# Retention and feed-forward in one kernel: items of a block taken as two, three and three instead of two at a time

## The chip, the cores and the metric

The kernel runs on one core of one Trainium2 chip. The metric is device microseconds of one execution. The core's engines are named as in the profile: PE (TensorE, matrix products; PEld is its loading of weights), DVE (VectorE), ACT (ScalarE), POOL (GpSimd) and SP (SyncE, which here issues nearly all DMAs). PE writes its results to PSUM, which has eight banks of 128 partitions x 512 fp32 values; DVE and ACT read them from there into SBUF.

## The reference, cut to what matters

```python
B, H, S, D = 8, 8, 576, 64
scores = matmul(q, k.transpose(0, 1, 3, 2)) / sqrt(D)
gamma = 1.0 - 2.0 ** (-5.0 - arange(H))
rel = arange(S)[:, None] - arange(S)[None, :]
Dmat = where(rel >= 0, gamma[:, None, None] ** rel, 0.0)
x = matmul(scores * Dmat, v)              # (B, H, S, D)
x = x.transpose(0, 2, 1, 3).reshape(B * S, H * D)     # 4608 x 512
h = x @ w_in                              # 512 x 2048
out = (h - tanh(h)) @ w_out               # 2048 x 512
```

All inputs are fp32. It is attention whose weights are scores times a decay that depends on the head and the distance, and a feed-forward layer behind it.

## The kernel before

**Blocks and items.** The sequence of 576 is cut into nine chunks of 64 positions. A *block* n is chunk n of all eight sequences: 512 tokens. An *item* j = 8 n + b is one sequence's chunk, with its eight heads: q, k, v and k by rows, 4 x 64 columns on 128 partitions each (two heads on top of each other). The decay is put into tables, so that within a block the scores need only a causal mask, and what earlier chunks contribute is one 64x64 *state* for each head, which grows by k'v of each chunk.

**The retention of an item** is three sorts of small products, each of 64x64 quarters of PE's array: *scores* (`m_score`, L220, 8 program matmuls), *states* (`m_state`, L226, 8) and *outputs* (`m_out`, L237, 16: state times q, and masked scores times v). Scores and states use the two quarters on the diagonal, outputs the two others; `run` (L247) issues two of the one and two of the other sort in turn, so that four quarters are at work. The profile shows every such matmul as two instructions.

**An entry** (`entry`, L289) does this for a pair of items: scores of the next pair, outputs and states of this one. Then DVE masks the scores (`after_score`, L255), ACT and DVE split the outputs into two words xh and xl (`after_out`, L276), DVE adds the states (L311), SP loads the pair after next (`load_pair`, L163, 1 MB, two buffers of the tag `a`), and POOL scales its q and v by tables (`prep`, L178). The table for q changes with the block: `load_qtab` (L155) loads it into one buffer.

**The feed-forward layer.** For block n and one of sixteen slices f of the inner dimension, `mm1(n, f)` (L320) makes h in a bank of the tag `h` (two buffers) with 12 matmuls of 128x128 by 512 columns: four parts of the contraction, and three products each, because weights and x are held as a high and a low word. `activate` (L345) turns h into g = h - tanh(h), again as two words gh and gl: tanh on ACT, subtraction on DVE, cast on ACT, subtraction on DVE. `mm2(n, f)` (L381) adds this slice's part of the result into four banks o0 to o3 with 12 matmuls. They go by word first (all of gh, then gl), except in a block's last mm2, where they go by bank, so that each bank is stored as it ends: `store` (L400) copies o0 and o2 on ACT, o1 and o3 on DVE, into tiles of the tag `cv` (three buffers), and SP stores them.

**The order of the work** is written out by hand, and `in_order` holds every engine's instructions to it. Each engine, and SP's queue of DMAs, does its instructions in that order and waits at one whose inputs or buffers aren't ready. It has three parts:

- The start and the loop over `seq` (L529): items of chunk 0, then mm1 of blocks 0 and 1 while the weights are loaded and converted. The 32 weight tiles arrive as 64-bit words of which the kernel makes two fp32 words (`guard`, L91: a mask, by tanh and abs on ACT; `unit`, L100: three bit operations on DVE, a cast on ACT, a subtraction on DVE). Entries for block 1 stand behind k = 5, 8, 10 and 14. h of both blocks is spilled to DRAM.
- The loop over `late` (L570): mm2 of block 1 and then of block 0, 32 in all, k from 0 to 31. Iteration k issues `words` for k + 1 (cast on ACT, subtraction on DVE, into gh and gl of two buffers each), `resume` for k + 2 (tanh on ACT, subtraction on DVE), the `fetch` for k + 4 on SP (256 KB from DRAM, three buffers of the tag `g`), what is left of the conversions, and mm2 of k. Block 1's last mm2, with its stores, is k = 15. Entries for block 2 stand ahead of mm2 at k = 3, 8, 13 and 18.
- The loop over blocks 2 to 8 (L586): mm1(n, f), then the mm2 of one f earlier; behind mm1 at f = 1, 5, 9 and 13 stands an entry for the next block, and the list `todo` holds what mm2 is still due.

Of the kernel before, what the change touches and what calls it, by code (L numbers as in the profile page):

```python
# [19 lines left out]
P = 128  # L20
NF = DF // P
NCC = DM // P
C = 64
# [4 lines left out]
HI_BITS = float(0x3FFFFF80)  # L28
# [5 lines left out]
NP = NC * B // 2  # L34
# [33 lines left out]
def retention_ffn(ctx: ExitStack, tc: tile.TileContext, ins, out, spill):  # L68
# [84 lines left out]
    loaded, scored, xs, qtabs = {}, {}, {}, {}  # L153
# [9 lines left out]
    def load_pair(p, u=None):  # L163

        if p >= NP:
            return
        c, pr = divmod(p, B // 2)
        load_qtab(c)
        a = loaded["pair", p] if u == 1 else pool.tile([P, 2, 4, 4, C], F32, tag="a", name=f"a{p}")
        if u is None:  # L170
            nc.sync.dma_start(a, qkv_d[c - 1, 2 * pr : 2 * pr + 2].rearrange("u p t i s -> p u t i s"))
        else:
            nc.sync.dma_start(a[:, u], qkv_d[c - 1, 2 * pr + u])
        loaded[2 * p], loaded[2 * p + 1] = a[:, 0], a[:, 1]
        loaded["pair", p] = a
        loaded["qv", p] = a[:, :, 0], a[:, :, 2]

    def prep(p, q=True):  # L178
        if p >= NP:
            return  # L180
        c = p // (B // 2)
        a = loaded["pair", p]
        if q:
            table = qtabs[c].unsqueeze(1).broadcast_to([P, 2, 4, C])
            nc.gpsimd.tensor_tensor(a[:, :, 0], a[:, :, 0], table, op=ALU.mult)  # L185
        nc.gpsimd.tensor_tensor(  # L186
            a[:, :, 2], a[:, :, 2], vtab[:, c].unsqueeze(1).unsqueeze(3).broadcast_to([P, 2, 4, D]), op=ALU.mult
        )

    def load_early(p):
        c, pr = divmod(p, B // 2)
        if pr < 2:
            return load_pair(p)
        src = qkv_d[c - 1, 2 * pr : 2 * pr + 2].rearrange("u p t i s -> p u t i s")
        parts = []
        for t in range(2):
            parts.append(const.tile([P, 2, 2, 4, C], F32, tag=f"wo{2 * (pr - 2) + t}", name=f"a_early{p}_{t}"))
            nc.sync.dma_start(parts[t], src[:, :, 2 * t : 2 * t + 2])  # L200
            behind(tc, pace[-1])
        for u in range(2):
            loaded[2 * p + u] = Parts([part[:, u] for part in parts])
        loaded["qv", p] = parts[0][:, :, 0], parts[1][:, :, 0]

    def scale_q(p):
        q, table = loaded["qv", p][0], qtabs[p // (B // 2)]
        nc.vector.tensor_tensor(q, q, table.unsqueeze(1).broadcast_to([P, 2, 4, C]), op=ALU.mult)

    def scale_v(p):  # L210
        v = loaded["qv", p][1]
# [25 lines left out]
    def m_out(j, o):  # L237
# [17 lines left out]
    def after_score(j, sc, n):  # L255
# [5 lines left out]
        else:  # L261
            pm = pool.tile([P, 2, 4, C], F32, tag="pm", bufs=1, name=f"pm{j}")
            nc.vector.tensor_tensor(
                pm[:, :n].rearrange("p u i q -> p (u i) q"), sc.rearrange("p u i q -> p (u i) q"),
                mask.unsqueeze(1).broadcast_to([P, 4 * n, C]), op=ALU.mult,
# [388 lines left out]
```

## Time and profile before

| | us |
|---|---|
| median of 3 runs | 891.48 (889.31 to 891.55) |
| the profiled execution | 891.8 |
| its span, first to last instruction | 890.0 |
| PE busy | 877.6 (99%) |
| PEld busy | 724.3 (81%) |
| DVE busy | 363.3 (41%) |
| ACT busy | 287.7 (32%) |
| POOL busy | 67.7 (8%) |
| granted PE clock, mean | 0.995 of full speed |

Times in rows are microseconds from the first instruction, and a row's second number is how long it took; groups show the mean of one in ns. An engine's row names the line, the operation, the tiles (out<-in) and their shapes; in brackets stands how long the engine stood idle before it and what ended that. A busy PE is not PE at its peak: matmuls overlap, and the distance from one start to the next is the price, not the length of the row.

### The profile page before, as it was taken

Reading aid. Unit: us, or ns where it says so; the run is one execution under the profiler, and the core shown is the slowest. Engines: PE = TensorE matmul, PEld = TensorE weight load, DVE = VectorE, ACT = ScalarE, POOL = GpSimd, SP = SyncE. Lnnn points to the kernel's source line nnn. Section 1 sums busy time; section 2 is a strip of 40 time slices with the busy share of each in tenths; the row PEclk is TensorE's granted clock in tenths of the full one; section 3 lists DMA queues with packets and bytes.
Section 4 is the critical chain, followed back from the end, with each engine's and each line's share of the span. In section 5 each row is a group of like instructions: output and inputs, shape, how many; then the busy total and the mean of one; then the engine's idle time right before and its main releaser. Section 6 shows DMA issues by size and latency. Waiting matters only on the chain.

```text
span 890.0 us, 17595 instructions
## 1 busy us (share of the span) xinstructions
PE 877.6 (99%) x7848; PEld 724.3 (81%) x7848; DVE 363.3 (41%) x548; ACT 287.7 (32%) x503; POOL 67.7 (8%) x59
## 2 busy tenths in 40 slices
PE   7999999999999999999999999999999999999997
PEld 6777878788888888888888888888888888888886
DVE  6879777653432332333233233323323322222222
ACT  4887774443222222222222222222222221222222
POOL 0001001210111110111111111111000111000000
PEclk8999999999999999999999999999999999999999
DMA  9966965551311131102111131113111201002001
GB/s 354 325 231 212 342 193 171 167 167 48 96 54 49 48 96 49 54 30 68 47 54 49 49 95 54 49 48 96 49 54 47 62 35 48 1 1 49 1 1 47
DMA packets 31372, 82.06 MB, mean 92 GB/s; under 512 B 3776, under 2 KB 4928, under 8 KB 31296
## 3 DMA queue, kind: packets, MB, share of 16 engines
q1 hardware_dynamic: 30768, 80.02, 27.8%
q8 instruction: 61, 1.00, 0.5%
q10 hardware_dynamic: 528, 0.92, 0.3%
q14 instruction: 15, 0.12, 0.0%
HBM read 63.62 MB, written 17.30 MB: 91 GB/s over the span
## 4 chain that ended last, share of the span: by engine, by line
PE 90%; DMA 3%; DVE 3%; ACT 2%; issue 0%; SPq 0%; DVEq 0%
PE o L393 44%; PE h L327 38%; PE s L252 3%; DMA rwo<-in_w_out_dram 2%; PE new L252 2%; PE own L252 2%; DMA rwi<-in_w_in_dram 1%; DVE mo L110 0%; DVE mo L112 0%; ACT mi L95 0%; ACT mi L98 0%; PE new_first L252 0%; DVE mi L105 0%; DVE wi L124 0%; ACT wi L117 0%
## 5 line engine op out<-in xcount | busy, mean ns | idle before, releaser
L327 PE MATMUL h<-xh,wi 128*128 128x512 f32 x1152 | 307.0, 392 | 2.7 <-ACT g L339 0.8
L393 PE MATMUL o<-wo,gh 128*128 128x512 f32 x1144 | 291.6, 393 | 0.4 <-DVE ob L412 0.4
L327 PEld LDWEIGHTS h<-xh,wi 128*128 128x128 f32 x1152 | 216.3, 189 | 49.7 <-ACT g L339 1.3
L393 PEld LDWEIGHTS o<-wo,gh 128*128 128x128 f32 x1144 | 212.3, 188 | 46.8 <-DVE ob L412 1.5
L354 DVE TENSOR_TENSOR g<-h,g 128x512 f32<-128x512 f32 x114 | 78.8, 691 | 367.1 <-ACT g L353 367.1
L353 ACT ACTIVATE g<-h 128x512 f32<-128x512 f32 x114 | 68.3, 599 | 420.9 <-PE h L327 420.1
L393 PE MATMUL o<-wo,gl 128*128 128x512 f32 x572 | 157.3, 389 | 0.0
L327 PE MATMUL h<-xl,wi 128*128 128x512 f32 x576 | 154.5, 390 | 0.0
L327 PEld LDWEIGHTS h<-xl,wi 128*128 128x128 f32 x576 | 108.7, 189 | 22.9
L393 PEld LDWEIGHTS o<-wo,gl 128*128 128x128 f32 x572 | 107.4, 188 | 22.3
L356 DVE TENSOR_TENSOR gl<-g,gh 128x512 fp32r<-128x512 f32 x113 | 81.0, 717 | 77.5 <-ACT gh L355 70.0
L355 ACT CAST gh<-g 128x512 fp32r<-128x512 f32 x113 | 70.1, 620 | 86.2 <-DVE g L354 86.2
L185 POOL TENSOR_TENSOR a<-a,qtab 128x512 f32<-128x512 f32 x27 | 36.3, 1344 | 605.7 <-DMA a<-in_qkv_dram 547.3
L252 PE MATMUL own<-a,state 64*64 64x64 f32 x960 | 58.9, 221 | 0.0
L252 PE MATMUL own<-pm,a 64*64 64x64 f32 x960 | 57.5, 218 | 0.0
L252 PEld LDWEIGHTS own<-a,state 64*64 64x64 f32 x960 | 47.8, 134 | 0.4 <-issue 0.4
L252 PEld LDWEIGHTS own<-pm,a 64*64 64x64 f32 x960 | 48.0, 135 | 0.0
L252 PEld LDWEIGHTS s<-a 64*64 64x64 f32 x960 | 30.3, 134 | 10.6 <-issue 10.2
L186 POOL TENSOR_TENSOR a<-a,vtab 128x512 f32<-128x512 f32 x28 | 32.2, 1152 | 67.4 <-DVE mi L112 67.4
L252 PE MATMUL s<-a 64*64 64x64 f32 x960 | 34.4, 221 | 0.0
L376 DVE TENSOR_TENSOR gl<-s,gh 128x512 fp32r<-128x512 f32 x30 | 21.6, 720 | 31.2 <-PE o L393 24.4
L375 ACT CAST gh<-s 128x512 fp32r<-128x512 f32 x30 | 18.6, 621 | 39.0 <-PE o L393 27.4
(67 smaller groups left out, 465.0 us busy)
## 6 DMA issues: line engine op xcount, KB each, us to landing
a<-in_qkv_dram SPq DMA_DIRECT2D x29, 1024.0 KB, 5.2
out_dram<-ob SPq DMA_DIRECT2D x69, 128.0 KB, 2.4
rwi<-in_w_in_dram SPq DMA_DIRECT2D x16, 512.0 KB, 5.8
rwo<-in_w_out_dram SPq DMA_DIRECT2D x16, 512.0 KB, 5.1
s<-spill_dram SPq DMA_DIRECT2D x30, 256.0 KB, 2.7
spill_dram<-g SPq DMA_DIRECT2D x20, 256.0 KB, 5.2
a<-in_first_dram SPq DMA_DIRECT2D x7, 384.0 KB, 5.0
spill_dram<-home SPq DMA_DIRECT2D x10, 256.0 KB, 6.3
```

The source lines that it names most:

```text
L185: nc.gpsimd.tensor_tensor(a[:, :, 0], a[:, :, 0], table, op=ALU.mult)
L186: nc.gpsimd.tensor_tensor(a[:, :, 2], a[:, :, 2], vtab[:, c].unsqueeze(1).unsqueeze(3).broadcast_to([P, 2, 4, D]), op=ALU.mult)
L252: nc.tensor.matmul(out_, w, x, start=start, stop=stop)
L327: nc.tensor.matmul(hp, win[f][:, a, cc, :], x[:, cc, :], start=(k == 0), stop=(k == 3 * NCC - 1))
L353: nc.scalar.activation(g, h, AF.Tanh)
L354: nc.vector.tensor_tensor(g, h, g, op=ALU.subtract)
L355: nc.scalar.copy(gh, g)
L356: nc.vector.tensor_tensor(gl, g, gh.bitcast(F32), op=ALU.subtract)
L375: nc.scalar.copy(gh, g)
L376: nc.vector.tensor_tensor(gl, g, gh.bitcast(F32), op=ALU.subtract)
L393: nc.tensor.matmul(ops[n][t], g[:, t * P : (t + 1) * P], wout[f_][:, a, :], start=(f_ == first and k == 0), stop=(f_ == final and k == 2),)
```

## The change

From block 2 on a block's items are taken as two, three and three (`entry3`) instead of four pairs. In a stretch of three, the third item's scores go first, into one half of a bank (`two`, in place of `new`) whose other half takes its outputs later; its states go into a bank of the tag `h`, and ACT copies them to SBUF (`kept`) so that the bank can take the next scores; its outputs are made last, beside the next stretch's scores. Stretches stand ahead of the work of k = 3, 13 and 20 in the `late` loop, and in blocks 2 to 7 behind mm1 and one mm2 at f = 2, 6 and 14, with one more mm2 behind them.

Loads are cut to match: a pair's q and k, and its v and k rows, are two DMAs of 512 KB each (tags `qk`, two buffers, and `vr`, one), a third item is one DMA of 512 KB (tag `one`, one buffer). POOL scales each part by itself. Masked scores are written over the k columns instead of into a tile of their own, and the tag `cv` has four buffers. Block 1's entries are as before.

The masks of weights: abs on ACT now writes fp32 with a scale whose bits are the whole mask, where it wrote int32 with a scale that is the mask as a number and so lacked its last bits.

```diff
-HI_BITS = float(0x3FFFFF80)
+HI_BITS = float(np.uint32(0x3FFFFFF8).view(np.float32))
...
-            masks[t, f] = pool.tile([P, DM], I32, tag="cv", bufs=3, name=f"m{t}{f}")
+            masks[t, f] = pool.tile([P, DM], I32, tag="cv", bufs=4, name=f"m{t}{f}")
...
-        nc.scalar.activation(masks[t, f], masks[t, f], AF.Abs, scale=HI_BITS)
+        nc.scalar.activation(masks[t, f].bitcast(F32), masks[t, f], AF.Abs, scale=HI_BITS)
...
-    def load_pair(p, u=None):
...
-    def prep(p, q=True):
...
+    def load_part(j, t):
+        if j >= NI:
             return
+        c, b = divmod(j, B)
+        if t == 0:
+            load_qtab(c)
+        early = c == 1 and b // 2
+        if early and early > 1:
+            part = const.tile([P, 2, 2, 4, C], F32, tag=f"wo{2 * (early - 2) + t}", name=f"early{j}_{t}")
+        elif early and t == 1:
+            part = pool.tile([P, 2, 2, 4, C], F32, tag="one", bufs=1, name=f"vr{j}")
+        else:
+            part = pool.tile([P, 2, 2, 4, C], F32, tag=("qk", "vr")[t], bufs=2 - t, name=f"{('qk', 'vr')[t]}{j}")
+        nc.sync.dma_start(part, qkv_d[c - 1, b : b + 2, :, 2 * t : 2 * t + 2].rearrange("u p t i s -> p u t i s"))
+        if early and early > 1:
+            behind(tc, pace[-1])
+        parts[j, t] = part
+        for u in range(2):
+            loaded.setdefault(j + u, Parts([None, None])).parts[t] = part[:, u]
+    def load_pair(j):
+        for t in range(2):
+            load_part(j, t)
+    def load_one(j):
+        c, b = divmod(j, B)
+        a = pool.tile([P, 4, 4, C], F32, tag="one", bufs=1, name=f"one{j}")
+        nc.sync.dma_start(a, qkv_d[c - 1, b])
+        loaded[j] = Parts([a[:, 0:2], a[:, 2:4]])
+        parts[j, 0], parts[j, 1] = a[:, 0:2].unsqueeze(1), a[:, 2:4].unsqueeze(1)
+    def prep(j, t, n=2):
+        if j >= NI:
             return
+        c = j // B
+        a = parts[j, t][:, :, 0]
+        if t == 0:
+            table = qtabs[c].unsqueeze(1).broadcast_to([P, n, 4, C])
+        else:
+            table = vtab[:, c].unsqueeze(1).unsqueeze(3).broadcast_to([P, n, 4, D])
+        nc.gpsimd.tensor_tensor(a, a, table, op=ALU.mult)
...
-    def m_out(j, o):
+    def m_out(j, o, state_last=False):
         c0, b = divmod(j, B)
         a, pm = loaded[j], scored[j]
         ms = []
         for i in range(4):
+            two = [[(o[half(1 - c), i], a[half(c), 2, i, :], pm[half(c), i, :]) for c in range(2)]]
             if c0 > 0:
-                ms += [(o[half(1 - c), i], state[half(c), b, i, :], a[half(c), 0, i, :], True, False) for c in range(2)]
-            ms += [(o[half(1 - c), i], a[half(c), 2, i, :], pm[half(c), i, :], c0 == 0, True) for c in range(2)]
+                two.insert(state_last, [(o[half(1 - c), i], state[half(c), b, i, :], a[half(c), 0, i, :]) for c in range(2)])
+            ms += [(*m, k == 0, k == len(two) - 1) for k, terms in enumerate(two) for m in terms]
         return ms
...
-            pm = pool.tile([P, 2, 4, C], F32, tag="pm", bufs=1, name=f"pm{j}")
+            pm = parts[j, 0][:, :, 1]
             nc.vector.tensor_tensor(
...
+                pm, sc, mask.unsqueeze(1).unsqueeze(1).broadcast_to([P, n, 4, C]), op=ALU.mult,
             )
...
-    def entry(p, sc, more=None):
...
+    def bank(name, tag):
+        return psp.tile([P, 2, 4, D], F32, tag=tag, bufs=2 if tag == "h" else 1, name=name)
+    def add_state(j, new, n=2):
+        st = state[:, j % B : j % B + n]
+        nc.vector.tensor_tensor(st, new, st, op=ALU.add)
+    def pair(what, j, bank):
+        return what(j, bank[:, 0]) + what(j + 1, bank[:, 1])
+    def entry(j, sc, more=None):
+        new, o = bank(f"new{j}", "new"), bank(f"own{j}", "own")
+        same, other = pair(m_score, j + 2, sc) + pair(m_state, j, new), pair(m_out, j, o)
...
+        after_score(j + 2, sc, 2)
+        after_out(j, o, 2)
+        add_state(j, new)
+    def entry3(j):
+        c0, b = divmod(j, B)
+        single, states = b > 0, c0 < NC - 1
+        then = j + 2 + single
+        o = bank(f"own{j}", "own")
+        outs, scores = pair(m_out, j, o), []
+        if single:
+            two = bank(f"two{j + 2}", "new")
+            run(m_score(j + 2, two[:, 1]), outs[:8])
+            after_score(j + 2, two[:, 1:], 1)
+            outs = outs[8:]
+            if states:
+                new = bank(f"new{j + 2}", "h")
+                run(m_state(j + 2, new[:, 0]), outs[:8])
+                outs = outs[8:]
+                kept = pool.tile([P, 1, 4, D], F32, tag="cv", bufs=4, name=f"kept{j + 2}")
+                nc.scalar.copy(kept, new[:, :1])
+        if states:
+            new = bank(f"new{j}", "h")
+            run(pair(m_state, j, new), outs[:16])
+            outs = outs[16:]
+        if single:
+            if not states:
+                run([], outs)
+            outs = m_out(j + 2, two[:, 0], True)
+            if states:
+                add_state(j, new)
+            low = after_out(j, o, 2, False)
+        if then < NI:
+            sc = bank(f"s{then}", "h")
+            scores = pair(m_score, then, sc)
+        run(scores, outs)
+        if not single:
+            if states:
+                add_state(j, new)
+            low = after_out(j, o, 2, False)
+        low()
+        if then < NI:
+            after_score(then, sc, 2)
+        if single:
+            if states:
+                add_state(j + 2, kept, 1)
+            after_out(j + 2, two[:, :1], 1)
+        more = then % B > 0
+        if then < NI:
+            load_part(then, 1)
+            prep(then, 1)
+            if more:
+                load_one(then + 2)
+                prep(then + 2, 1, 1)
+                prep(then + 2, 0, 1)
+            load_part(then + 2 + more, 0)
+            prep(then + 2 + more, 0)
...
-            load_pair(B, k - 9)
+            load_part(first, k - 9)
...
         if k == 14:
-            load_pair(B + 1)
-        if k in (26, 28):
-            prep(B + (k - 26) // 2, k == 28)
-    p = B
+            load_part(first + 2, 0)
+        if k == 26:
+            prep(first, 1)
+        if k == 28:
+            prep(first + 2, 0)
     for k, (n, f) in enumerate(late):
+        if k in (3, 13, 20):
+            entry3(first + (0, 2, 5)[(3, 13, 20).index(k)])
         if 0 < k < len(late) - 1:
             words(*late[k + 1])
         if k < len(late) - 2:
...
             fetch(*late[k + 4])
         for _ in range(2 if k < 4 else 1):
             step()
-        if k in (3, 8, 13, 18):
-            entry(p, psp.tile([P, 2, 4, C], F32, tag="h", bufs=2, name=f"s{n}_{f}"))
-            p += 1
         if k < len(late) - 1:
             mm2(n, f)
...
     for n in range(2, NC):
         for f in range(NF):
             mm1(n, f)
-            if n + 1 < NC and f % 4 == 1:
-                sc = psp.tile([P, 2, 4, C], F32, tag="h", bufs=2, name=f"s{n}_{f}")
-                entry((n + 1) * B // 2 + f // 4, sc)
             todo.append((n, f))
-            if (n, f) != (NC - 1, NF - 2):
+            if len(todo) > 1 and (n, f) != (NC - 1, NF - 2):
+                mm2(*todo.pop(0))
+            if n + 1 < NC and f in (2, 6, 14):
+                entry3((n + 1) * B + (0, 2, 5)[(2, 6, 14).index(f)])
                 mm2(*todo.pop(0))
```

More of the change, by code (lines that the diff above doesn't have):

```diff
@@ L150, in units @@
             step()
-    loaded, scored, xs, qtabs = {}, {}, {}, {}
+    loaded, scored, xs, qtabs, parts = {}, {}, {}, {}, {}
     def load_qtab(c):
@@ L178, in prep @@
-    def prep(p, q=True):
-        if p >= NP:
-            return
[L181 to L204, printed above, removed]
@@ L287, in first_states @@
         return ms, lambda: nc.scalar.copy(state[:, b : b + 2], new)
-    def entry(p, sc, more=None):
-        c0, pr = divmod(p, B // 2)
-        new = psp.tile([P, 2, 4, D], F32, tag="new", bufs=1, name=f"new{p}")
-        o = psp.tile([P, 2, 4, C], F32, tag="own", bufs=1, name=f"own{p}")
-        same, other = [], []
-        for u in range(2):
-            if p + 1 < NP:
-                same += m_score(2 * p + 2 + u, sc[:, u])
-            other += m_out(2 * p + u, o[:, u])
-        if c0 < NC - 1:
-            for u in range(2):
-                same += m_state(2 * p + u, new[:, u])
+    def bank(name, tag):
[8 more added lines that the diff above has]
+        same, other = pair(m_score, j + 2, sc) + pair(m_state, j, new), pair(m_out, j, o)
         if more is not None:
@@ L528, in retention_ffn @@
     scales = {2: 4, 4: 5, 7: 6, 9: 7, 13: 8}
+    first = 2 * B
     for k, (n, f) in enumerate(seq):
@@ L533, in retention_ffn @@
         if k + 1 in early:
-            scale_v(early[k + 1])
+            scale_v(2 * early[k + 1])
         if last_two < 0:
@@ L555, in retention_ffn @@
             behind(tc, pace[-1])
-            sc = scores_of(B // 2 - 1)
+            sc = scores_of(3)
             ms, done = first_states(0, "new")
-            run(m_score(B, sc[:, 0]) + m_score(B + 1, sc[:, 1]) + ms, [])
+            run(pair(m_score, B, sc) + ms, [])
             after_score(B, sc, 2)
```

47 lines of the change are left out of this document (13 added, 34 removed).

## The prediction

> **What bounds the kernel now.** I read the profile's page first, then the chain of waits in order of time.
>
> ```profile
> span 890.0 us, 17595 instructions
> PE 877.6 (99%) x7848; PEld 724.3 (81%) x7848; DVE 363.3 (41%) x548; ACT 287.7 (32%) x503; POOL 67.7 (8%) x59
> ```
>
> PE is never long without work, so a change counts only if PE issues less, or stands still. The chain of one period (four mm1, four mm2, one entry) is PE alone; of its eight groups the first and the last:
>
> ```profile
> 229.08 2.95 PE o L393 x12
> ...
> 248.35 2.72 PE h L327 x12
> ...
> 253.09 1.12 PE o L393 x4
> ```
>
> From 229.08 to 253.09 are 24.01 us. Eight groups of twelve matmuls at 2.72 make 21.76; the entry costs the remaining 2.25 us, which includes the 0.23 by which the first group after it is longer than 2.72. PE's timeline says what lies in it (the second and the last of 32 rows of the diagonal half, each row with its partner of the other half):
>
> ```profile
> 251.11 0.23 PE L252 MATMUL s<-a 64*64 64x64 f32 x2
> ...
> 252.86 0.23 PE L252 MATMUL new<-a 64*64 64x64 f32 x2
> ```
>
> Thirty steps in 1.75 us are 0.0583 each, 32 are 1.87. So 2.25 - 1.87 = **0.38 us of an entry depend on no matmul**: they are paid for going into the 64x64 form and out. The waits list agrees on where: the first weight load of the small form stands idle some 0.35 us (10.6 over 30 entries).
>
> ```profile
> PEld s L252 <- issue: 10.6, 30, 0.4
> ```
>
> **The change part by part.**
>
> *Fewer entries.* A block's 8 items go through PE in three stretches instead of four. The small matmuls are as many as before (32 program matmuls an item, in fours), and the lone ones of the last block too (80 outs without a partner, before and after). What goes is one entry per block, in blocks 2 to 8: 7 x 0.38 = **2.7 us off**.
>
> *Four buffers instead of three for masks, tanh and output tiles.* At the one boundary of blocks that has no entry behind it, the copy of the fourth output tile waits until the first tile's store has landed and frees a buffer:
>
> ```profile
> 800.45 5.19 SPq L414 DMA_DIRECT2D out_dram<-ob  x8
> ...
> 803.20 0.84 PE L393 MATMUL o<-wo,gh 128*128 128x512 f32 x3
> ...
> 803.46 0.69 DVE L412 COPY ob<-o 128x512 f32<-128x512 f32 x1 [2.20 <-PE h L327]
> ...
> 804.21 1.45 PE L393 MATMUL o<-wo,gh 128*128 128x512 f32 x5 [0.16 <-DVE ob L412]
> ```
>
> Three matmuls from 803.20 should end in the fourth at 803.88; it starts at 804.21, and the restart costs about 0.1 more. A fourth buffer removes this: **0.4 us off**. At the other boundaries an entry covered the same wait before; now the entry stands one pair of f later, and without the fourth buffer each of six would pay the 0.4.
>
> *Waits inside a stretch of three.* The third item's scores take 8 steps (8 x 0.058 = 0.47 us), its states 0.47, the pair's states 0.93, and then come its outputs with the next scores. Two things must be ready for those: its masked scores, and the bank of its states, copied to SBUF by ACT. The nearest rows of that size:
>
> ```profile
> L260 DVE TENSOR_TENSOR pm<-s_first,decay 128x256 f32<-128x256 f32 x8 | 3.4, 423 | 6.5 <-PE s_first L252 6.0 <-PE own_first L252 0.3
> ...
> L278 ACT CAST xh<-own_first 128x256 fp32r<-128x256 f32 x8 | 2.9, 364 | 2.4 <-PE own_first L252 2.4
> ```
>
> With 0.23 us until a small matmul has ended and 0.06 for each of two signals (as between the copy's end at 804.15 and PE's start at 804.21), the mask is there after 0.77 of 1.40 us, the copy after 0.71 of 0.93. Both fit, the copy with 0.2 us to spare; what hides them is the pair's states. I take nothing. Without that cover the copy would cost 0.7 in each of the 12 stretches that have it. Below nothing it can't go, as there is no wait of before to remove.
>
> *The order of mm1 and mm2.* After each entry the new loop empties its list, so the next two mm1 stand side by side, and their first mm2 comes 2.72 us after its mm1 instead of 5.44. Between lie a tanh, a subtraction, a cast and a second subtraction; from PE's first slot behind an mm1 to the end of the last of them:
>
> ```profile
> 245.47 1.98 PE L393 MATMUL o<-wo,gh 128*128 128x512 f32 x8
> ...
> 247.68 0.69 DVE L356 TENSOR_TENSOR gl<-g,gh 128x512 fp32r<-128x512 f32 x1 [0.69 <-ACT gh L355]
> ```
>
> That is 2.90 us. The plain mm2 wants this last result only for its ninth matmul, 2.72 + 8 x 0.227 = 4.5 us on; a block's last mm2, whose order is another, for its third, 3.17 us on, less a weight load ahead of it. I take 0.2 for six blocks together, between 0 and 1.
>
> *The load of the queries' table in the `late` loop (mm2 of blocks 1 and 0).* This is the step that decides. Block 2's stretch at k = 13 loads, on SP and in this order: v and k rows of the next pair, all of the single item behind it, the next block's table, the next block's first q and k. The table has one buffer, whose last reader is now the scaling of that single item on POOL, which is loaded one instruction earlier. So SP stands until that load has landed and POOL has scaled it, and the fetch for k = 17, which used to be issued ahead of the entry, stands behind. Before:
>
> ```profile
> 165.61 0.32 SPq L363 DMA_DIRECT2D s<-spill_dram  x1
> ...
> 166.02 0.39 SPq L161 DMA_DIRECT2D qtab<-in_qtab_dram  x1
> ...
> 166.74 2.11 PE L393 MATMUL o<-wo,gh 128*128 128x512 f32 x8
> ...
> 172.14 0.63 ACT L368 ACTIVATE th<-s 128x512 f32<-128x512 f32 x1
> ...
> 172.92 1.50 POOL L185 TENSOR_TENSOR a<-a,qtab 128x512 f32<-128x512 f32 x1 [12.90 <-DMA a<-in_qkv_dram]
> ...
> 173.19 0.59 ACT L410 COPY ob<-o 128x512 f32<-128x512 f32 x1 [0.43 <-PE o L393]
> 173.19 1.78 DVE L369 TENSOR_TENSOR s<-s,th 128x512 f32<-128x512 f32 x1
> ...
> 174.90 1.28 DVE L412 COPY ob<-o 128x512 f32<-128x512 f32 x2
> 175.03 0.39 PE L393 MATMUL o<-wo,gh 128*128 128x512 f32 x1
> ...
> 175.64 2.02 PE L393 MATMUL o<-wo,gh 128*128 128x512 f32 x7 [0.21 <-DVE ob L412]
> ```
>
> The tanh at 172.14 is that of k = 17. Behind it in ACT's order, and behind its subtraction (173.19) in DVE's, stand the copies that free block 1's output banks, and the first mm2 of block 0 waits for those. Sizes and landing times, and POOL's prices for two items:
>
> ```profile
> a<-in_qkv_dram SPq DMA_DIRECT2D x29, 1024.0 KB, 5.2
> ...
> rwo<-in_w_out_dram SPq DMA_DIRECT2D x16, 512.0 KB, 5.1
> s<-spill_dram SPq DMA_DIRECT2D x30, 256.0 KB, 2.7
> ...
> qtab<-in_qtab_dram SPq DMA_DIRECT2D x8, 128.0 KB, 2.4
> ```
>
> ```profile
> L185 POOL TENSOR_TENSOR a<-a,qtab 128x512 f32<-128x512 f32 x27 | 36.3, 1344 | 605.7 <-DMA a<-in_qkv_dram 547.3 <-PE h L327 44.1 <-ACT wo L117 14.4
> L186 POOL TENSOR_TENSOR a<-a,vtab 128x512 f32<-128x512 f32 x28 | 32.2, 1152 | 67.4 <-DVE mi L112 67.4
> ```
>
> Let E be the first matmul behind the entry (166.74 above). A load of 512 KB lies between 2.7 (256 KB) and 5.2 (1024 KB) by size, while the weights' 5.1 comes from crowded stretches; on the line between the quiet rows it lands after 3.5. The single item's buffer is free at E, so it lands at E+3.6, when POOL is done with the pair's rows; two scalings of one item at half price, 0.6 and 0.7, end at E+5.0. Table, next q and k, then the fetch are issued at 0.4 each: the fetch at E+5.8, landed with 3.0 (256 KB behind larger ones) at E+8.8. Tanh 0.63 to E+9.5; the subtraction meets POOL's scaling of the next q and k, as at 173.19, and takes 1.2 instead of 0.7: E+10.7; DVE's two copies, 1.3: E+12.0. The fourth matmul of block 0's first mm2 needs the second of them. Undisturbed it would start 3 x 0.227 after 175.03, at E+9.0; before, that mm2 was already 0.4 late (175.64 instead of 175.26). **Added: 12.0 - 9.0 - 0.4 = 2.6 us**. With every load at the low end (2.7) and no meeting with POOL it is 1.0; with 5.2 for the load, 4.3. In blocks 3 to 8 SP waits there as well, but nothing is queued behind that is due before the next block. That SP stands for the table until POOL has read the old one is in the queue's own waits already:
>
> ```profile
> SPq L161 <- POOL a L185: 34.2, 5, 7.6
> ```
>
> A rule of the Trainium skill speaks against this part. DMA: Bandwidth & Descriptors, sections "Anatomy of one DMA" and "Measured", has each (there on GpSimd's path) transfer pay about 2.0 us fixed besides bytes at 436 GB/s, and wants transfers of 1 MiB. By it the halved loads land after an estimated 3.2 us, not 3.5, and the added stall is 2.3. The trace's 5.2 for 1024 KB is longer than its 4.4.
>
> *Entries ahead of words and resume in the `late` loop.* At k = 3 the conversions still occupy DVE, and the entry's three DVE operations (of 512 elements, some 0.7 each like the copy at 803.46) now stand ahead of the next words and of the resume; and three loads bring POOL operations that meet DVE's. I take 0.4, between 0 and the 1.1 of one such meeting (1.78 for 0.69, as at 173.19).
>
> *The rest.* Full masks: the same 32 ACT operations, another output type. Two more DMA issues early, 0.4 each, while weights are queued far ahead. Masked scores written over the k columns: same elements. Half a megabyte less to load ahead of the `late` loop. Together nothing, between -0.8 and +0.8 (two issues either way); what hides it is PE's backlog of mm1.
>
> *Sum.* -2.7 - 0.4 + 2.6 + 0.2 + 0.4 = +0.1 us. The profiled execution takes 891.8 (span 890.0 and 1.8 around it), so 891.9; it lies 0.3 above the median of 891.48, so I forecast **891.6**. Here 0.3% is 2.7 us, about what a measurement of this kernel can tell from no change.
>
> **The rivals.**
>
> *The fetch is in time.* If loads land quicker, or the old table is let go earlier, the stall at k = 16 doesn't come: 891.5 - 3.1 + 0.6 = 889.0, or 888.4 without the 0.6 of small terms. For it speaks that fetches are issued four k ahead and SP waited 7.6 us elsewhere for nothing; against it that ACT's order puts the copies behind this very tanh. Chance 0.28.
>
> *The stall costs PE its clock, and the kernel is slower.* The windows view near the start has this:
>
> ```profile
> 11.40:14.80 3.40, 1.69 (x75) 1.42 (x77) 2.93 (x9) 1.39 (x4) 0.00 (x0) 1.00 1.04 392
> 14.80:18.20 3.40, 2.81 (x33) 2.41 (x30) 3.00 (x7) 3.26 (x7) 0.00 (x0) 0.50 0.99 387
> ```
>
> After 3.4 us in which PE was busy for 1.69, the granted clock was 0.50 for the next 3.4 us. My stall leaves PE about 2.6 us idle within 3.5. Where that falls into one such stretch, the next one, or the next two if the first doesn't give the clock back, run at half speed and lose 1.7 us each: 893.3 or 895.0. Slower by 0.3% it is from the second stretch on, or when the fetch lands after about E+10 with one. Against it: the stall may be split over two stretches, and the early matmuls are small ones. Chance 0.27, half of it beyond 0.3%. The Trainium skill, TensorE: Matmul & The Clock Gate, section "Why this matters for your kernels", asks for a gap of over about 3 us before the clock falls. By that rule this rival needs a longer stall than mine; the window above, half busy, fell without one.
>
> *A longer hold of SP.* With 6 us per load and POOL's operations stretched the added stall is above 5: 894 and over. Chance 0.05.
>
> **How the numbers follow.** Forecast 0.40 (its own range 890.0 to 893.3), rivals 0.28, 0.27 and 0.05. Faster by over 0.3% (below 888.8) needs the first rival with its small terms at zero or "the rest" on the good side, over half of it: 0.16. Slower by over 0.3% (above 894.2): half of the second and most of the third, 0.17. Same: 0.67. The range, 888.2 to 894.6, takes in the first rival with its small terms at zero, and the second with one slow stretch.
>
> **What would show it.** Three L252 stretches a block from block 2 on; one period of a three-item stretch longer than a two-item one by about 0.94 us; 23 entries in the PEld wait instead of 30; no wait for the third item's mask or copy. At k = 13 of the late loop the table's issue 5 us behind the entry's end with POOL as releaser, the tanh of k = 17 waiting for its DMA, the output copies behind it, PE idle before the first mm2 of block 0; the granted clock behind that. Wrong it is if that tanh doesn't wait, or if PE waits inside the stretches.

## The result, and the profile after

The changed kernel takes 895.24 us (median of 8 runs, 892.89 to 896.48), beside 890.14 us for the kernel before on the same chip (8 runs, 888.90 to 891.55): a ratio of 1.0056, 95% interval 1.0043 to 1.0069. It is slower by 5.1 us, where 0.1 us more had been forecast. In two later sets of 30 and 25 runs the kernel before had medians of 889.46 and 889.34.

The page of the changed kernel, first lines:

```profile
span 893.0 us, 17735 instructions
PE 874.8 (98%) x7848; PEld 723.6 (81%) x7848; DVE 368.8 (41%) x568; ACT 293.5 (33%) x522; POOL 70.3 (8%) x73
```

PE has the same 7848 matmuls and is busy for 2.8 us less, and the span is 3.0 us longer. So PE stands still somewhere. Three points on PE's timeline cut the span into parts: the first mm2 of the `late` loop, the first mm1 of block 2, the last three matmuls. Before:

```profile
124.53 1.75 PE L393 MATMUL o<-wo,gh 128*128 128x512 f32 x7
...
218.74 1.07 PE L327 MATMUL h<-xh,wi 128*128 128x512 f32 x4
...
884.62 0.84 PE L393 MATMUL o<-wo,both 128*128 128x512 f32 x3
```

After:

```profile
122.23 1.98 PE L451 MATMUL o<-wo,gh 128*128 128x512 f32 x8
...
224.58 1.07 PE L385 MATMUL h<-xh,wi 128*128 128x512 f32 x4
...
887.75 0.84 PE L451 MATMUL o<-wo,both 128*128 128x512 f32 x3
```

- Up to the `late` loop: 124.53 before, 122.23 after, 2.3 less. This goes with the clock, not with the change: the profiled execution before had its clock at half from 14.8 to 21.6 us (the windows view in the prediction has the first of the two rows), and that after had it at 1.00 there; later runs of the kernel before with a mean clock of 1.000 span 886.8 to 887.8 us, and the profiled one, with 0.995, spans 890.0. Without this difference the two profiled executions stand 5.3 us apart, about as the medians do.
- The `late` loop: 94.21 before, 102.35 after, **8.14 more**.
- Blocks 2 to 8: 665.88 before, 663.17 after, **2.71 less**.

The loss is all in the `late` loop, at the place that the prediction named. E, the first matmul behind the stretch at k = 13, is now at 163.58. SP's timeline, with the instruction's start and the time that its issue took:

```profile
162.84 0.38 SPq L179 DMA_DIRECT2D vr<-in_qkv_dram  x1
163.79 0.71 SPq L193 DMA_DIRECT2D one<-in_qkv_dram  x1
170.66 0.33 SPq L162 DMA_DIRECT2D qtab<-in_qtab_dram  x1
171.04 0.43 SPq L179 DMA_DIRECT2D qk<-in_qkv_dram  x1
171.56 1.36 SPq L421 DMA_DIRECT2D s<-spill_dram  x3
```

From 164.5 to 170.66 SP issues nothing. It stands for the table (L162), and three fetches stand behind. The row of SP's waits names the releaser, the scaling of the single item:

```profile
SPq L162 <- POOL one L207: 34.2, 6, 6.1
```

POOL's timeline has that scaling's end, 169.90 + 0.73 = 170.63, just ahead of the table's issue:

```profile
167.35 1.57 POOL L207 TENSOR_TENSOR vr<-vr,vtab 128x512 f32<-128x512 f32 x1 [24.61 <-DMA vr<-in_qkv_dram]
168.88 1.06 POOL L207 TENSOR_TENSOR one<-one,vtab 128x256 f32<-128x256 f32 x1
169.90 0.73 POOL L207 TENSOR_TENSOR one<-one,qtab 128x256 f32<-128x256 f32 x1
```

The DMA view of 160 to 180 us gives KB each and the median time to landing in the last two columns:

```profile
s<-spill_dram SPq DMA_DIRECT2D x3, 256.0 KB, 5.5
vr<-in_qkv_dram SPq DMA_DIRECT2D x1, 512.0 KB, 4.3
one<-in_qkv_dram SPq DMA_DIRECT2D x1, 512.0 KB, 4.7
qk<-in_qkv_dram SPq DMA_DIRECT2D x1, 512.0 KB, 5.2
```

A fetch now lands 5.5 us after its issue; it took 2.7 before. ACT's and DVE's timelines go on from there:

```profile
176.92 0.63 ACT L426 ACTIVATE th<-s 128x512 f32<-128x512 f32 x1 [6.75 <-DMA s<-spill_dram]
177.46 1.05 ACT L468 COPY ob<-o 128x512 f32<-128x512 f32 x2
...
177.58 0.69 DVE L427 TENSOR_TENSOR s<-s,th 128x512 f32<-128x512 f32 x1 [6.40 <-ACT th L426]
178.19 1.28 DVE L470 COPY ob<-o 128x512 f32<-128x512 f32 x2
```

ACT was idle for 6.75 us for the fetch; the copies of block 1's output banks come right behind its tanh and its subtraction. PE waits for them with the first mm2 of block 0 (E is the first row):

```profile
163.58 2.11 PE L451 MATMUL o<-wo,gh 128*128 128x512 f32 x8
...
171.65 0.39 PE L451 MATMUL o<-wo,gl 128*128 128x512 f32 x1
178.08 4.21 PE L451 MATMUL o<-wo,gh 128*128 128x512 f32 x8 [6.04 <-ACT ob L468]
...
183.28 2.01 PE L451 MATMUL o<-wo,gh 128*128 128x512 f32 x8
```

That mm2 starts 6.2 us late (171.65 + 0.23 to 178.08), and its twelve matmuls take 5.20 us, to 183.28, instead of 2.72. The windows view (PE busy is the third number, the granted clock the one behind POOL's) says why:

```profile
172.40:175.80 3.40, 0.00 (x0) 0.00 (x0) 0.00 (x0) 0.00 (x0) 0.00 (x0) 1.00 0.95 266
175.80:179.20 3.40, 1.06 (x2) 0.56 (x3) 1.62 (x3) 2.28 (x5) 1.27 (x1) 0.50 0.28 108
179.20:182.60 3.40, 3.40 (x9) 2.63 (x10) 1.47 (x3) 0.64 (x2) 0.00 (x0) 0.50 0.68 157
```

From 172.4 to 175.8 no engine does anything, while the DMA engines are busy for 95% of the time. Behind that the clock is 0.50 for 6.8 us.

### The profile page after: what moved, and what is told of

Read it like the earlier page. It is cut to its first block, busy times and chain, and to the rows that moved or that the text cites. A ratio compares the mean times of both kernels' runs of the same rounds, so it can differ in the third digit from the quotient of the medians.

```text
span 893.0 us, 17735 instructions
## 1 busy us (share of the span) xinstructions
PE 874.8 (98%) x7848; PEld 723.6 (81%) x7848; DVE 368.8 (41%) x568; ACT 293.5 (33%) x522; POOL 70.3 (8%) x73
## 4 chain that ended last, share of the span: by engine, by line
PE 85%; DMA 5%; DVE 4%; ACT 3%; issue 1%; POOL 0%; SPq 0%; DVEq 0%; POOLq 0%; ACTq 0%
PE o L451 42%; PE h L385 36%; DMA rwo<-in_w_out_dram 2%; PE new L257 2%; PE s L257 2%; PE own L257 1%; PE two L257 1%; DMA rwi<-in_w_in_dram 1%; DMA s<-spill_dram 1%; DVE mo L111 0%; DMA vr<-in_qkv_dram 0%; DVE mo L113 0%; DVE s L427 0%; DVE mo L106 0%; DMA spill_dram<-g 0%
## 5 line engine op out<-in xcount | busy, mean ns | idle before, releaser
L385 PE MATMUL h<-xh,wi 128*128 128x512 f32 x1152 | 302.4, 390 | 2.9 <-issue 1.1
L207 POOL TENSOR_TENSOR vr<-vr,vtab 128x512 f32<-128x512 f32 x21 | 23.1, 1100 | 626.9 <-DMA vr<-in_qkv_dram 540.9
L257 PE MATMUL own<-qk,state 64*64 64x64 f32 x736 | 45.2, 221 | 0.0
L257 PE MATMUL own<-qk,vr 64*64 64x64 f32 x736 | 44.1, 218 | 0.0
L257 PEld LDWEIGHTS own<-qk,vr 64*64 64x64 f32 x736 | 36.8, 135 | 0.0
L257 PEld LDWEIGHTS own<-qk,state 64*64 64x64 f32 x736 | 36.7, 134 | 0.0
L207 POOL TENSOR_TENSOR qk<-qk,qtab 128x512 f32<-128x512 f32 x20 | 27.7, 1385 | 46.7 <-DMA qk<-in_qkv_dram 46.7
L427 DVE TENSOR_TENSOR s<-s,th 128x512 f32<-128x512 f32 x30 | 22.7, 757 | 8.1 <-ACT th L426 8.1
L257 PE MATMUL s<-qk 64*64 64x64 f32 x736 | 25.5, 219 | 0.0
```

The lines of the kernel that those rows point to most:

```text
L207: nc.gpsimd.tensor_tensor(a, a, table, op=ALU.mult)
L257: nc.tensor.matmul(out_, w, x, start=start, stop=stop)
L385: nc.tensor.matmul(hp, win[f][:, a, cc, :], x[:, cc, :], start=(k == 0), stop=(k == 3 * NCC - 1))
L427: nc.vector.tensor_tensor(g, g, th, op=ALU.subtract)
```

## The experiments

My theory: SP's stand for the table, with the fetch behind it, and the half clock that follows are the whole loss; the rest of the change gains some 3 us. Rival 1: not the stand but the bytes queued ahead of the fetch, and beside it, make it late. Rival 2: the order on ACT and DVE is the cause, since the entry now stands ahead of words and resume. "Late loop" below is the time between the first two of the points above: 94.21 us before, 102.35 after.

**The table without its late reader.**

```diff
-                prep(then + 2, 0, 1)
+                if then + 2 != 2 * B + 7:
+                    prep(then + 2, 0, 1)
```

> Only the scaling of the single item's q on POOL at k = 13 is left out (that item's q stays unscaled), so the table has no late reader and SP needn't stand for it; the three loads are still queued ahead of the fetch for k = 17. Theory (SP stands for the table, the fetch behind it): the table's issue follows the loads at once, the fetch is issued some 5 us earlier, the stall at the first mm2 of block 0 is gone with the half clock behind it, the late loop from the first late mm2 to mm1(2,0) falls from 102.4 to 94 to 95 us, the time to 887 to 888 (-7.5 to -8 against the changed kernel). Rival 1 (not the wait but the loads ahead of the fetch and their company make it late): the fetch still lands 5 us after its issue and most of the stall stays, 893 to 895. Rival 2 (the entry's ACT and DVE work ahead of words and resume is the cause): stall unchanged, 895.

Measured: 888.27 us (12 runs), ratio 0.9984 (0.9974 to 0.9995); late loop 96.20. PE and ACT at the place:

```profile
173.48 0.49 PE L452 MATMUL o<-wo,gh 128*128 128x512 f32 x1 [1.51 <-ACT ob L469]
```

```profile
172.32 0.63 ACT L427 ACTIVATE th<-s 128x512 f32<-128x512 f32 x1 [2.22 <-DMA s<-spill_dram]
```

This kernel leaves one item's q unscaled. Without the stand the late loop gets back 6.15 of its 8.14 us, and the clock stays at 1.00; 94 to 95 had been expected. But the tanh still waits for its DMA, and a stall of 1.5 us is left. The fetch was issued at 165.94 and reached the tanh at 172.32, 6.4 us later, behind 1.6 MB of loads. So the theory holds for the larger part, and rival 1 has a part that I had given to nobody.

**The loads behind the fetch, the entry's work left where it is.** The entry hands its loads back, and the loop writes them one line later:

```diff
-            entry3(first + (0, 2, 5)[(3, 13, 20).index(k)])
+            loads = entry3(first + (0, 2, 5)[(3, 13, 20).index(k)])
...
             fetch(*late[k + 4])
+        if k in (3, 13, 20):
+            loads()
```

> The whole computation; in the late loop the entry's loads and scalings are written behind the fetch, its ACT, DVE and TensorE work stays ahead of words and resume. Theory: SP stands for the table as long as now (some 5 us), but nothing urgent is behind it; the tanh of k = 17 waits for no DMA, no stall, 887 to 888. Rival 1 expects the same here (fetch ahead of the loads). Rival 2 (ACT and DVE order): stall stays, 894 to 895.

Measured: 893.57 us (12 runs), ratio 1.0040 (1.0027 to 1.0054); late loop 100.53. The tanh of k = 17 waits for no DMA, as expected, but neither the 887 to 888 of the theory nor the 894 to 895 of rival 2 came. SP:

```profile
168.20 0.41 SPq L193 DMA_DIRECT2D one<-in_qkv_dram  x1
175.27 0.33 SPq L162 DMA_DIRECT2D qtab<-in_qtab_dram  x1
175.65 0.67 SPq L179 DMA_DIRECT2D qk<-in_qkv_dram  x1
176.41 0.89 SPq L426 DMA_DIRECT2D s<-spill_dram  x2
```

and ACT:

```profile
181.48 0.63 ACT L431 ACTIVATE th<-s 128x512 f32<-128x512 f32 x1 [7.70 <-DMA s<-spill_dram]
```

The stand is as long as ever, from 168.6 to 175.27. The fetch for k = 17 is ahead of it now, and the stall has moved to the next one: the mm2 that needs k = 18 stood for 4.4 us, and the clock fell for 3.4. The waiting tanh names a DMA, which speaks against rival 2, though the next run gives the order on ACT and DVE a part. My step "nothing urgent is behind it" was wrong: a fetch is issued at each k, every 2.7 us, so a queue that stands for over 6 us always holds one.

**The whole entry behind words, resume and fetch**, as the kernel before had it:

> The whole computation; in the late loop the whole entry goes where the kernel before had it, behind words, resume and fetch. Theory: the same as with the loads alone moved, less the small wait at k = 3 (some 0.4): 886.6 to 887.6, below the kernel before (890.1) by 2.5 to 3.5. If the order of ACT and DVE was a large part of the loss, it is better than the run with the loads alone moved by more than 1 us.

Measured: 888.49 us (12 runs), ratio 0.9982 (0.9973 to 0.9992); late loop 96.77. The stand is still there (5.9 us, from 163.23 to 169.15), and so is a stall, of 1.3 us at k = 18. The late loop is 3.8 us shorter than with the loads alone moved, so by the sign set ahead (more than 1 us) the order of ACT and DVE was a large part of what that run lost. The entry's DVE operations no longer stand ahead of the one that frees a fetch's buffer, so the fetches are issued earlier (two from 157.91 to 160.95, there from 160.08 to 167.61) and have more in hand when SP stands. The order thus decides how much of the stand reaches PE; what it costs where SP doesn't stand, the two runs with the table at k = 15 show below.

**PE kept busy through the wait.**

```diff
+        if k == 15:
+            spare = psp.tile([P, BLK], F32, tag="new", bufs=1, name="spare")
+            for i in range(22):
+                nc.tensor.matmul(spare, win[i % 8][:, 0, 0, :], wout[i % 8][:, 0, :], start=True, stop=True)
```

> The changed kernel with 22 spare 128x512 matmuls (5.0 us at 0.227) ahead of block 0's first mm2, their result not used: TensorE works while it waits for the output copies. Theory (half clock behind the stall is a term of its own, from 178.1 to 182.6 us at 0.50, 2.2 us lost): the granted clock stays at 1.00 there, the copies end as late as now, and the time falls by 1.9 to 2.3 to about 893.2. Rival (the slow matmuls behind the stall wait for late data, the clock is a label): no gain, 895.

Measured: 893.44 us (7 runs), ratio 1.0045 (1.0028 to 1.0062); late loop 99.99, 2.36 less. PE:

```profile
171.54 5.15 PE L646 MATMUL spare<-wo,wi 128*128 128x512 f32 x22
176.84 0.50 PE L451 MATMUL o<-wo,gh 128*128 128x512 f32 x1 [0.16 <-ACT ob L468]
...
180.47 1.75 PE L451 MATMUL o<-wo,gh 128*128 128x512 f32 x7
```

The clock stays at 1.00, and the mm2 takes 3.63 us (176.84 to 180.47) instead of 5.20. So the half clock is a term of its own, **1.6 us**. The medians alone couldn't tell, as the two ratios' intervals overlap (1.0043 to 1.0069 for the changed kernel). The other 0.8 of the 2.36 is the wait itself, which was 5.3 us in this run instead of 6.2: the fetch landed after 4.4 us here, after 5.3 there. With 11 spare matmuls:

> The changed kernel with 11 spare matmuls (2.5 us) instead of 22 ahead of block 0's first mm2, their result not used; some 3 to 3.7 us of the wait stay idle. If the clock falls for the stretch of 3.4 us behind one that was less than half busy, it falls here for at most one stretch (as with 0.44 of 3.40 busy where the q and k load was put behind the fetch), and the time lies between the two: profile 0.9 to 1.7 us above the one with 22. If what counts is an unbroken idle time of 3.4 us, it stays at 1.00 or falls by where the stretches lie; then it is the same as with 22.

```profile
174.20:177.60 3.40, 0.28 (x2) 0.00 (x0) 0.41 (x1) 1.07 (x3) 1.26 (x1) 1.00 0.76 265
177.60:181.00 3.40, 3.25 (x7) 2.28 (x8) 2.68 (x5) 1.57 (x4) 0.00 (x0) 0.50 0.56 131
```

Measured: 893.79 us (one run, the profiled one); late loop 101.45, 1.46 more than with 22. About 1.0 of that is the clock (the mm2 takes 4.64 instead of 3.63), the rest a longer wait. The clock falls for one stretch of 3.4 us, behind one in which PE was busy for 0.28, although PE's longest idle time was 3.21: no unbroken 3.4 us are needed.

**Table ahead of the fetch, the next block's q and k (512 KB) behind it.**

> The whole computation, the entry where the change puts it; in the late loop the table (and SP's wait for POOL ahead of it) stays ahead of the fetch for k = 17, only the next block's q and k rows (512 KB) go behind the fetch. Theory as the first four runs leave it (SP's wait sets when the fetch is issued, the bytes queued with it set when it lands): the fetch is issued some 0.5 us earlier and lands after 3 to 3.5 us instead of 5.3, the stall at block 0's first mm2 shrinks from 6.2 to 3.4 to 4 us; if the clock still falls 892.5 to 893, if it holds 890.5 to 891. Rival (company costs nothing, landing is a fixed time): the stall shrinks by 0.5 only, 894.5.

Measured: 891.39 us (10 runs), ratio 1.0017 (1.0006 to 1.0029); late loop 98.10. The fetch for k = 17 landed after 2.7 us, and the wait of PE shrank from 6.04 to 2.96. The company had cost 2.6 us of the landing, a little more than the 1.8 to 2.3 expected, and the rival (a fixed landing time) falls. The clock fell for one stretch, and the time came out below what was expected for that case: the landing was quicker, block 0's first mm2 took 4.75 us instead of 5.20 with one slow stretch in place of two, and a wait of 0.4 us at k = 7 was gone:

```profile
171.30:174.70 3.40, 0.44 (x2) 0.19 (x1) 0.72 (x2) 1.38 (x3) 0.00 (x0) 1.00 0.92 277
174.70:178.10 3.40, 3.16 (x8) 2.19 (x8) 2.79 (x4) 1.36 (x3) 1.74 (x1) 0.50 0.94 286
```

**Table and next q and k at k = 15.** All else as in the changed kernel; `rest` is a function that the entry hands back, with the table's load, q's and k's, and their scaling:

```diff
-            entry3(first + (0, 2, 5)[(3, 13, 20).index(k)])
+            rest = entry3(first + (0, 2, 5)[(3, 13, 20).index(k)])
+            if k != 13:
+                rest()
...
             fetch(*late[k + 4])
+        if k == 15:
+            rest()
```

> The whole computation; of the changed kernel only this is different: table and next block's q and k of the stretch at k = 13 are written behind the fetch at k = 15. By then POOL is done with the single item, so SP doesn't stand for it. The two 512 KB loads are still ahead of the fetch for k = 17. Theory: no stand of SP over 1 us in that place, stall at block 0's first mm2 below 1.5 us, clock 1.00, the late loop 94.5 to 95.5 us, 887 to 888 beside 889.5 for the kernel before. If the two loads' company alone makes the fetch late, as where the table's wait was taken out (1.9 us of stall left): 888.5 and more.

Measured: **887.22 us** (11 runs), ratio 0.9970 (0.9958 to 0.9982); late loop 95.13. SP:

```profile
163.43 0.87 SPq L193 DMA_DIRECT2D one<-in_qkv_dram  x1
165.65 5.53 SPq L426 DMA_DIRECT2D s<-spill_dram  x3
171.27 0.38 SPq L162 DMA_DIRECT2D qtab<-in_qtab_dram  x1
```

The three fetches go out one by one in the time in which SP stood, and the table then waits for nobody. This one move brings back 7.2 us of the late loop, and by the two ratios (1.0056 to 0.9970) 7.7 us of the time. The move takes away the stand and the 640 KB ahead of the fetch at once. How the two share is read from the first run (stand gone, bytes left: 6.15 back) and from the one before this (stand left, 512 KB gone: 4.25 back, 0.4 of it at k = 7). The two overlap, as together they are more than the whole 8.14, and they leave little for any other cause.

**The same, with the entries at k = 3 and k = 13 behind words, resume and fetch.**

> The whole computation; as the run before, and the entries at k = 3 and k = 13 behind words, resume and fetch. Then the fetch for k = 17 is ahead of all loads and the next one is behind 1 MB only. Theory: no stall over 0.5 us left in the late loop, which takes 93.8 to 94.3 us; with the 2.7 us that blocks 2 to 8 gain, 886.3 to 887 beside 889.5 for the kernel before (ratio 0.9965 to 0.9972). Rival (something else that the change adds costs 1 to 2 us more): 888 and over, as where the entry alone was moved.

Measured: **886.32 us** (9 runs, 885.32 to 888.70), ratio **0.9962** (0.9949 to 0.9976); late loop 93.79, about before's 94.21 less the 0.38 of the one entry saved there. This version beats both kernels. The order on ACT and DVE, which is what it changes against the run before, is worth 1.34 us of the late loop (95.13 to 93.79); with that and the table moved, nothing else in the change costs anything that these runs can tell.

**Spare stretches of small matmuls**, in the version of 886.32 us, to see the price of the form itself:

```diff
+            if n + 1 < NC and f in (4, 10):
+                spare = bank(f"spare{n}_{f}", "new")
+                for i in list(range(4)) * (1 if f == 4 else 4):
+                    for c in range(2):
+                        nc.tensor.matmul(spare[half(c), 0, i], state[half(c), 0, i, :], state[half(c), 0, i, :], start=True, stop=True)
```

> The kernel with the table at k = 15 and words first, and in blocks 2 to 7 two more stretches of small matmuls each: 4 steps of 64x64 behind f = 4, 16 steps behind f = 10, with a spare output. Theory (0.38 us for going into the small form and out, 0.0585 a step): 0.61 us and 1.32 us added to the pitch of the big matmuls around them, together 11.6 us for the twelve. Rival (the change of form is nothing, the gain of blocks 2 to 8 has another source): 0.23 and 0.94, 7.0 us together.

PE around one short and one long stretch (the big matmuls ahead of it, and those behind):

```profile
242.80 1.07 PE L390 MATMUL h<-xh,wi 128*128 128x512 f32 x4
243.80 0.68 PE L662 MATMUL spare<-state 64*64 64x64 f32 x16
244.41 2.11 PE L456 MATMUL o<-wo,gh 128*128 128x512 f32 x8
...
279.47 1.07 PE L390 MATMUL h<-xh,wi 128*128 128x512 f32 x4
280.46 2.08 PE L662 MATMUL spare<-state 64*64 64x64 f32 x64
282.48 2.11 PE L456 MATMUL o<-wo,gh 128*128 128x512 f32 x8
```

Four matmuls at 0.227 from 242.80 end the old pitch at 243.71; the next mm2 starts at 244.41, 0.70 later, and its own eight take 2.11 instead of 1.98: 0.83 us. The long stretch costs 2.10 and 0.13, 2.23. My expected sizes were wrong, since I had counted two program matmuls to a step, as in an entry, where those on the diagonal have a partner on the other quarters; here they have none, and the 8 and 32 program matmuls (16 and 64 instructions) are 8 and 32 steps, not 4 and 16. From the two, a step is (2.23 - 0.83) / 24 = 0.058, and 0.83 - 8 x 0.058 leaves **0.36 us that depend on no matmul**, beside 0.38 in the prediction. Rival ("the change of form is nothing") falls. The profiled run took 909.85 us, 23.5 more; 18.4 are these twelve stretches, and most of the remainder are three stretches of three items with 0.9 to 1.4 us of waiting each, for which the profile names no releaser, and a half clock at the start.

**Three buffers instead of four**, in the version of 886.32 us:

> The kernel with the table at k = 15 and words first, with three buffers instead of four for masks, tanh, output tiles and the kept states. Prediction's step: at each boundary of blocks from block 2 on the fourth output tile's copy waits for a store, 0.4 us of TensorE's time each, seven in all, 2.6 to 3.1 us. Rival (the stores are done before the copy, now that an entry's place is another): only the last boundary pays, 0.4.

```profile
225.06 0.84 PE L456 MATMUL o<-wo,gh 128*128 128x512 f32 x3
226.14 1.20 PE L456 MATMUL o<-wo,gh 128*128 128x512 f32 x4 [0.24 <-DVE ob L475]
```

Measured: 890.79 us (one run). This is the first of seven such waits, one at each boundary of blocks, 0.31 to 0.45 us each, 2.7 together. From mm1 of block 2 to the last matmuls it takes 666.90 us instead of 663.28, 3.6 more, so the restart behind each wait costs about 0.1 on top. The rival (one boundary alone) falls.

## Why the prediction was wrong

*Right, and measured as forecast.* Fewer entries and the fourth buffer: -2.71 us in blocks 2 to 8, where six entries (2.3) and one wait (0.4) stand in the sum; the price of an entry was taken apart with the spare stretches, that of the buffer with three buffers. The Trainium skill, TensorEngine Tiling (Array Packing), section "Key Properties", says that a change of tiling mode drains the engine, without a price; the 0.36 agree with it. No wait inside the stretches of three in blocks 3 to 8; one of them:

```profile
264.00 1.07 PE L451 MATMUL o<-wo,gl 128*128 128x512 f32 x4
...
267.96 2.11 PE L451 MATMUL o<-wo,gh 128*128 128x512 f32 x8
```

264.91 to 267.96 and 0.13 are 3.18 us, 48 steps of 0.0583 and 0.38. The mm1 side by side were put at 0.2 for blocks 2 to 8, and PE waits nowhere there: 0.

*Right in size by luck: the 0.4 for the entry ahead of words at k = 3.* It was put down to the entry's DVE operations and to POOL. What came late is the mm2 of k = 7, by 0.4 us (144.06 instead of 143.65):

```profile
144.06 2.12 PE L451 MATMUL o<-wo,gh 128*128 128x512 f32 x8 [0.25 <-ACT gh L433]
```

The tanh ahead of it had waited 0.88 us for a fetch that was issued at 136.65, behind the stretch's three loads (1.5 MB), and landed after 4.8 us; a subtraction that met POOL (1.17 us instead of 0.69) added to it. With the q and k load behind the fetch, that mm2 was on time. So the term was the company of a load once more, in small.

*Wrong: the term of +2.6 for the table's load in the `late` loop.* The mechanism was the right one, instruction by instruction, and its size was not:

| relative to E | forecast | measured |
|---|---|---|
| single item landed | 3.6 | 4.9 |
| POOL done with it | 5.0 | 7.1 |
| fetch issued | 5.8 | 8.0 |
| fetch landed | 8.8 | 13.3 |
| tanh done | 9.5 | 14.0 |
| subtraction done | 10.7 | 14.7 |
| DVE's copies done | 12.0 | 15.9 |

With the same 9.0 and 0.4 taken off, 15.9 makes 6.5 us of added stall. The largest part of the 3.9 is the fetch's landing: taken at 3.0, measured at 5.3, behind table, q and k (640 KB), which were issued within the microsecond ahead of it. With q and k behind the fetch it took 2.7. Next is the single item's load, taken at 3.5 and measured at 4.7, behind another 512 KB; and POOL took 2.1 from there instead of 1.4. Only the subtraction's meeting with POOL didn't come, which gave back 0.5. The single item's load had been read off a line between sizes, as if it travelled alone; the fetch had been given 0.3 us for its company, which cost 2.6; and the range of the term (1.0 to 4.3) varied the single item's load and the meeting with POOL, not the fetch's company.

*Two rivals came together.* The longer hold of SP, which had 0.05, asked for an added stall above 5 us and 894 or more: it was 6.5 us, by a load of 4.7, POOL at 2.1 and a fetch of 5.3, not by 6 us per load. And the lost clock, which had 0.27, came with it: the stall left one stretch of 3.4 us empty and most of the next (PE busy for 1.06), and the clock was at half for two. I had priced two slow stretches at 3.4 us and got 895.0; they cost 1.6, since PE stood for the first 2.3 us of them anyway. That 895.0 is near the 895.24 measured is thus luck, made of a stall too short and a clock too dear. Together, 6.5 + 1.6 + 0.4 - 0.4 = 8.1 in the late loop, where 2.6 + 0.4 - 0.4 had been put.

*The base.* Two of the three runs that the forecast stood on were above 891, and the profiled one had its clock at half for 6.8 us near the start. Later sets have the kernel before at 889.3 to 890.1. The forecast time, 891.6, is therefore only 3.6 us below the measured one; the forecast difference was off by more: 0.1 us beside 5.1.

The cited estimate of the Trainium skill (3.2 us for a load of 512 KB) is further from the measured 4.3 and 4.7 than my 3.5. Its rule on the clock, in TensorE: Matmul & The Clock Gate, section "Why this matters for your kernels", asks for no gap over about 3 us: the gaps of 6.04, 4.42, 3.21 and 2.96 us lost the clock here, those of 1.51 and 1.29 didn't, so it agrees for this loop. At the start of four of the profiled executions the clock fell with no gap above 2.2 us, so there it doesn't; the last section has what does fit.

## What to carry to other kernels

When a change adds a wait to a queue, list everything that is issued through that queue while it stands, not just the next instruction: here each k had its fetch, so moving one of them only handed the stall to the next. Time a load by the bytes that were issued ahead of it and haven't landed, and not by its own size alone; here 512 KB issued behind it didn't slow it. Then move what waits (the table and what comes with it) to a place where its releaser is long done: two steps of the loop later turned this change from a loss of 0.56% into a gain of 0.30%, and of 0.38% with the entries behind words, resume and fetch.

## What the runs showed that I had not expected

The same 256 KB fetch landed after 2.5 to 2.8 us when alone or ahead of a load, after 3.5 when issued behind 1 MB that was half landed, after 4.4 to 6.1 right behind 640 KB (five executions, 5.3 in the changed kernel's), and 6.4 behind 1.6 MB.

The granted clock fell for stretches of 3.4 us, in the late loops behind one in which PE was busy for 0.00, 0.28 or 0.44 us. The start of the kernel before, where it fell behind a stretch busy for 1.69, is the same thing, once the stretches are counted from the moment at which the clock changed. Six of the profiled executions have such a moment. In them the clock fell behind all eight full-speed stretches in which PE was busy for 1.70 us or less of 3.41 (0.00 to 0.45 in the late loops, 1.16 to 1.70 at the start), and behind none in which it was busy for 2.05 or more; none lies between. A slow stretch was followed by another when PE was busy for 1.10 or 2.83 us of it, and by the full clock when it was busy for 2.95 or more. Where the clock fell twice in one execution, at 14.29 and 174.70 us in one and at 16.10 and 183.35 in another, the two moments lie 47 and 49 times 3.413 us apart, so the stretches seem to follow a fixed grid. On its own grid the changed kernel's profiled execution had no start stretch below 2.07, and the clock held there. So in these traces it is the share of a stretch that decides, with the limit near a half, and not an unbroken gap. How the grid lies in an execution, no run here sets.
